# Attention ahead of a mixture of experts: the first two blocks in an order written out, zero products on TensorE, and the output bank put into the rotation

## The chip, the cores and the metric

One core of one Trainium2 chip runs the whole program. The metric is the device time of one execution in microseconds (us), as the median of three runs. Five engines work side by side on the core and meet by semaphores: TensorE (PE, with its weight loads as PEld), VectorE (DVE), ScalarE (ACT), GpSimd (POOL) and SyncE (SP), which issues most of the transfers.

## The reference

Attention with four sink positions and a window of 128 runs over 4 batches, 8 heads, 768 positions and 64 numbers a head. Its output, 3072 rows of 512, goes through eight experts, whose weights for each row come from a gate that is normalised over rows and columns.

```python
scores = scale * np.matmul(q, k.transpose(0, 1, 3, 2))
keep = is_sink | in_window            # 4 sinks, the last 128 positions
scores = np.where(keep, scores, -1e9)
a = np.exp(scores - np.max(scores, axis=-1, keepdims=True))
a = a / (np.sum(a, axis=-1, keepdims=True) + 1e-09)
x = np.matmul(a, v)                   # then reordered to rows of 512

P = np.exp(x @ w_gate - max)          # normalised over rows and columns, 8 times
for e in range(8):
    h = np.maximum(x @ w1[e], 0.0)
    out += P[:, e:e + 1] * (h @ w2[e])
```

## The kernel before

The attention is cut into 24 blocks: four batches of six blocks of 128 queries. A block has eight heads, in two halves of four; half `hh` of block `m` has the number 2m + hh, and "scores 5" below means the second half of block 2. For each half, in this order: TensorE transposes keys and queries (L451), ACT and DVE write them as a high and a low part (`split_qk`, L459 and L460), TensorE multiplies them (`scores`, L482, one bank a head), DVE folds the window (L491) and adds the mask and takes the maximum (L492), ACT takes the exponential (L494), DVE adds and inverts the sums (`scaled`, L500 and L501), POOL scales the four heads (L503), TensorE transposes the result (`transpose_p`, L514), ACT copies it out (PT, L515), POOL cuts a triangle from it (PC, L517), and TensorE multiplies by the values (`values`, L559) into one output bank, O. When both halves are in, the sink part is added (`sink_values`, L567), and `store_x` copies O out, half on ACT (L575) and half on DVE (L576, `xr`). The sinks' own values are written as high and low parts once for each batch (`split_sinks`, L418 and L419, on POOL).

No scheduler moves anything: the order in each engine's queue is the order of the code. The code goes in rounds. In the steady part, round m (from 4 on) holds the scores of block m+1, the values of block m-1, the gate products of an earlier block, the transposes of keys and queries of block m+2 and of the weights of block m, the sinks and the store of block m-1, and last the **fill**: four steps of `plain()`, the first expert's work written as a generator. The fill of a round is either one second-layer product (L640, `plain_g2`, one bank, 12 products of 512 columns) or two first-layer products (L625, `plain_g1`, two banks of 12 products of 256 columns each; call the banks c0 and c1). Each first-layer bank is later read by DVE for the low part of the hidden layer (`h`, L631). Before round 4 there are shorter rounds of half a block each.

TensorE's results go to eight banks. `new_bank` takes the first of the list `banks` and puts it back at the list's end at once, so a bank comes up again eight requests later, and whoever writes it then waits for its last reader. A bank taken with `keep` stays out of the list until it is put back by hand:

```python
    def new_bank(shape, keep=False):
        j = banks.pop(0)
        if not keep:
            banks.append(j)
```

The output bank O is taken that way (L552), and `store_x` puts it back (L572).

After the attention the other seven experts run as products of sums of blocks; that part is not touched.

## Time and profile before

| | |
|---|---|
| median of 3 runs | 2093.32 us (2093.08 to 2093.78) |
| the profiled execution's own time | 2093.69 us |
| its span in the trace | 2091.9 us |
| TensorE busy in the span | 2063.7 us, 99% |
| DVE, ACT, POOL busy | 1473.7, 842.9, 711.7 us |
| the attention with the first expert | from the start to some 260 us |

The span is what the trace shows from the first instruction to the last; 1.8 us of the execution's own time lie around it. TensorE's share of 99% is an average over 2091.9 us: the first 60 us, where the attention starts up and nothing else is there to multiply, look different, and all of TensorE's idle time that matters lies there and at single places of the rounds.

### The profile page before, as it was taken

To read this page: it belongs to the slowest core of one execution; us is meant where nothing else is said; L and a number is where in the kernel's file an instruction comes from. 1 tells how busy PE (TensorE), PEld (TensorE's weight loads), DVE (VectorE), ACT (ScalarE), POOL (GpSimd) and SP (SyncE) were. 2 spreads that over 40 slices of the span, in tenths; PEclk is the share of its full clock that TensorE was granted. 3 is DMA by queue.
4 is the path that set the end of the run, shared out by engine and by line. 5 is a ranking of instruction groups with operands and counts; after the bars stand their busy time and mean duration, and the time that the engine had idled before them with its cause. 6 is when DMAs were issued, how large, how long until landed. Compare 5 with 4: busy or idle time off the path is not lost.

```text
span 2091.9 us, 31617 instructions
## 1 busy us (share of the span) xinstructions
PE 2063.7 (99%) x10561; PEld 1714.7 (82%) x10561; DVE 1473.7 (70%) x2762; ACT 842.9 (40%) x1799; POOL 711.7 (34%) x839
## 2 busy tenths in 40 slices
PE   7999999999999999999999999999999999999998
PEld 6888888888888888888888888888888888888887
DVE  7767697877777776856666666666766666666666
ACT  6877545444444444432233323322432332233222
POOL 6765533332323221332223222323322232223223
PEclk9999999999999999999999999999999999999999
DMA  7655249898989887676666666668766666666662
GB/s 162 155 124 115 87 142 333 292 312 288 321 273 333 274 278 257 236 247 197 203 201 196 201 205 196 201 205 324 235 206 195 198 209 192 201 207 199 196 197 85
DMA packets 397624, 453.82 MB, mean 217 GB/s; under 512 B 99664, under 2 KB 265744, under 8 KB 396560
## 3 DMA queue, kind: packets, MB, share of 16 engines
q1 hardware_dynamic: 397064, 451.57, 68.6%
q8 instruction: 87, 1.43, 0.3%
q14 instruction: 81, 0.66, 0.1%
q10 hardware_dynamic: 392, 0.16, 0.0%
HBM read 314.17 MB, written 137.46 MB: 216 GB/s over the span
## 4 chain that ended last, share of the span: by engine, by line
PE 95%; DVE 3%; ACT 0%; issue 0%; POOL 0%; DMA 0%; SPq 0%; DVEq 0%; POOLq 0%; ACTq 0%
PE c L875 41%; PE o L1439 21%; PE held L1439 8%; PE held L1125 7%; PE o L1125 7%; PE st L625 2%; PE st L640 2%; PE st L559 2%; PE st L482 1%; PE st L451 1%; DVE sc L492 1%; PE st L514 1%; DVE st L491 1%; PE st L567 0%; PE st L591 0%
## 5 line engine op out<-in xcount | busy, mean ns | idle before, releaser
L901 ACT CAST hf<-w 128x512 fp32r<-128x512 f32 x448 | 265.1, 621 | 563.5 <-POOL w L1406 300.7
L1439 PE MATMUL o<-hf,W2q 128*128 128x512 f32 x1920 | 472.1, 390 | 0.0
L1439 PEld LDWEIGHTS o<-hf,W2q 128*128 128x128 f32 x1920 | 360.2, 188 | 75.3 <-DVE acc L1453 0.9
L875 PE MATMUL c<-T,W1q 128*128 128x512 f32 x1530 | 389.0, 390 | 0.2 <-DVE w L1387 0.2
L904 DVE TENSOR_TENSOR hf<-w,hf 128x512 fp32r<-128x512 f32 x448 | 330.6, 766 | 76.6 <-ACT hf L901 69.5
L875 PEld LDWEIGHTS c<-T,W1q 128*128 128x128 f32 x1530 | 286.9, 188 | 60.6 <-DVE w L1387 0.9
L1453 DVE TENSOR_TENSOR acc<-o,acc 128x512 f32<-128x512 f32 x298 | 204.8, 688 | 168.9 <-PE o L1439 168.9
L875 PE MATMUL c<-B,W1q 128*128 128x512 f32 x1134 | 278.4, 390 | 0.0
L1406 POOL TENSOR_TENSOR w<-w 128x512 f32<-128x512 f32 x64 | 82.7, 1292 | 492.5 <-DVE w L1388 492.5
L875 PEld LDWEIGHTS c<-B,W1q 128*128 128x128 f32 x1134 | 212.6, 188 | 43.9
L1387 DVE TENSOR_TENSOR w<-c,M 128x512 f32<-128x512 f32 x192 | 132.4, 689 | 138.4 <-PE c L875 133.9
L1383 ACT COPY M<-c 128x512 f32<-128x512 f32 x192 | 112.8, 587 | 248.1 <-PE c L875 248.0
L1439 PE MATMUL held<-hf,W2q 128*128 128x512 f32 x768 | 194.8, 390 | 0.0
L1125 PE MATMUL held<-W2f,h 128*128 128x512 f32 x672 | 171.2, 390 | 0.0
L875 PE MATMUL c<-T,W1f 128*128 128x512 f32 x672 | 171.0, 390 | 0.1
L1125 PE MATMUL o<-W2f,h 128*128 128x512 f32 x672 | 170.6, 390 | 0.1
L1439 PEld LDWEIGHTS held<-hf,W2q 128*128 128x128 f32 x768 | 144.1, 188 | 29.8
L1421 POOL TENSOR_TENSOR w<-w 128x512 f32<-128x512 f32 x64 | 105.6, 1650 | 176.2 <-DVE hf L904 176.2
L1125 PEld LDWEIGHTS o<-W2f,h 128*128 128x128 f32 x672 | 126.0, 188 | 26.9 <-DVE acc L1132 0.9
L875 PEld LDWEIGHTS c<-T,W1f 128*128 128x128 f32 x672 | 125.9, 188 | 26.6 <-issue 0.5
L1125 PEld LDWEIGHTS held<-W2f,h 128*128 128x128 f32 x672 | 125.9, 188 | 26.4 <-DVE W2f L904 0.5
L1410 POOL TENSOR_TENSOR w<-w 128x512 f32<-128x512 f32 x64 | 83.8, 1309 | 176.3 <-DVE w L1388 172.1
(210 smaller groups left out, 2700.2 us busy)
## 6 DMA issues: line engine op xcount, KB each, us to landing
W2q<-w2s SPq DMA_DIRECT2D x448, 256.0 KB, 3.1
W1q<-w1s SPq DMA_DIRECT2D x444, 256.0 KB, 2.8
w1s<-W1f SPq DMA_DIRECT2D x56, 896.0 KB, 6.8
w2s<-WT SPq DMA_DIRECT2D x136, 256.0 KB, 3.8
r<-in_moe_w_dram SPq DMA_DIRECT2D x64, 512.0 KB, 3.7
w2s<-W2f SPq DMA_DIRECT2D x56, 256.0 KB, 5.4
PB<-psd SPq DMA_DIRECT2D x16, 512.0 KB, 3.7
w2s<-W2f SPq DMA_DIRECT2D x56, 128.0 KB, 6.8
```

The source lines that it names most:

```text
L559: nc.tensor.matmul(O[r * D:(r + 1) * D, c], lhsT=x_[:, 2 * c + r], rhs=y_[:, 2 * c + r], start=(j == 0 and c == 0), stop=(j == len(ops) - ...
L875: nc.tensor.matmul(ps, lhsT=w1(a, k), rhs=x[:, b, k, :], start=(start and j == 0), stop=(stop and j == len(TERMS) - 1), skip_group_check=n ...
L901: nc.scalar.copy(dst[:, 0], src)
L904: low_ = nc.vector.tensor_sub(dst[:, 1], src, f32(dst[:, 0])).ins
L1125: nc.tensor.matmul(o, lhsT=h[c, th][:, a, off:off + P], rhs=W2F[n][:, w, c, :], start=(begin and c == 0 and j == 0), stop=(end and c == 1 ...
L1383: nc.scalar.copy(t, T["c2"])
L1387: nc.vector.tensor_add(w, T["c1"], T[m])
L1406: nc.gpsimd.tensor_sub(S3, T["A11"], T["A21"])
L1410: nc.gpsimd.tensor_add(T["A21"], T["A21"], T["A22"])
L1421: at(k, lambda: nc.gpsimd.tensor_sub(T["A11"], w, T["A11"]))
L1439: nc.tensor.matmul(o, lhsT=W2Q[part, n, m][:, a, k * P:(k + 1) * P], rhs=F[part, n, H_OF[m]][:, w, :], start=(j == 0 and (begin or not hol ...
L1453: nc.vector.tensor_add(sums[m, k], o, sums[m, k])
```

## The change

Blocks 0 and 1, and the scores of block 2's first half, leave the loop over rounds and stand as one sequence ahead of it, in which the values of all four halves and both stores come ahead of scores 4. In this sequence, `idle(k)` issues k products of a zero tile by itself into a bank of its own (`zeros`, kept out of the list until the loop's fourth round). The high and low parts of the sinks are written by DVE and no longer by POOL, for later batches by way of `pending`, which the code empties after the next round's second head. The output bank is taken in turn, without `keep`, where both halves' values stand in one round. Four steps of the fill that stood in the last rounds stand in the loop's first, ahead of its values; the number of steps is the same. `small_products` uses three slots of its bank and not two, and the sums of the gate's rows (`add_up_rows`) come later.

```diff
+    zero = attc.tile([P, P], F32, name="zero")
+    nc.vector.memset(zero, 0.0)
...
     def split_sinks(b):
         VS = seq[b] = att.tile([SK, H * D], F32R, name="VS")
         vmf = vms[b].rearrange("p h d -> p (h d)")
-        nc.gpsimd.tensor_scalar(VS, vmf, 1.0, 1.0, op0=ALU.mult, op1=ALU.mult)
-        nc.gpsimd.tensor_sub(VS[2 * NK:], vmf[2 * NK:], f32(VS[2 * NK:]))
+        nc.vector.tensor_copy(VS, vmf)
+        nc.vector.tensor_sub(VS[2 * NK:], vmf[2 * NK:], f32(VS[2 * NK:]))
...
-    def transpose_qk(m, hh):
+    def transpose_qk(m, hh, gap=0):
...
+                idle(gap * (pr == j == 0))
...
-        t = new_bank([P, HH, P])
+        t = u["pt", hh] = new_bank([P, HH, P])
         for h in range(HH):
             nc.tensor.transpose(t[:, h, :], u["sc"][:, hh * HH + h, SINK:], ident)
-        nc.scalar.copy(u["PT"][0][:, hs], t)
-        if i:
+
+    def copy_p(m, hh):
+
+        u = us[m]
+        hs = slice(hh * HH, (hh + 1) * HH)
+        nc.scalar.copy(u["PT"][0][:, hs], u["pt", hh])
...
-        tsk = new_bank([P, 2, P])
+        tsk = new_bank([P, 3, P])
...
-    def values(m, hh):
+        for j, (t, ls) in enumerate(sums):
+            nc.vector.tensor_copy(Pt[:, t, :], tsk[:, 1 + j, 0:E])
+
+    def values(m, hh, keep=True):
 
         u = us[m]
         if hh == 0:
-            u["O"], u["bank"] = new_bank([P, KC, P], True)
+            u["O"], u["bank"] = new_bank([P, KC, P], True) if keep else (new_bank([P, KC, P]), None)
...
     def store_x(m):
         b, i = spans[m]
-        banks.append(us[m]["bank"])
+        if us[m]["bank"] is not None:
+            banks.append(us[m]["bank"])
...
+    FIRST = 4
...
-    for n in range(-2, 2 * HALF + 1):
-        new_qk = {-2: [0, 1], -1: [], 0: [2, 3]}.get(n, [n + 3])
-        rounds.append(([n + 1] if n >= -1 else [], new_qk, [n] if n >= 0 else [], 2 if n >= 5 else 0, 1 if n >= 1 else 0))
-    rounds.append(([2 * HALF + 2, 2 * HALF + 3], [2 * HALF + 4, 2 * HALF + 5], [2 * HALF + 1], 4, 2))
+    for n in range(FIRST, 2 * HALF + 1):
+        rounds.append(([n + 1], {4: [6], 5: [7, 8]}.get(n, [n + 3]), [n], (4, 0) if n == FIRST else (0, 2), 2))
+    rounds.append(([2 * HALF + 2, 2 * HALF + 3], [2 * HALF + 4, 2 * HALF + 5], [2 * HALF + 1], (0, 4), 2))
     for m in range(HALF + 1, L + 3):
         both = lambda j: [2 * j, 2 * j + 1] if j < L else []
-        rounds.append((both(m + 1), both(m + 2), both(m), {L: 2, L + 1: 2, L + 2: 0}.get(m, 4), 2))
-    begin = {0: 0, HALF + 1: len(rounds) - (L + 2 - HALF)}
-    at_block = lambda m: begin[HALF + 1] + m - HALF - 1
+        rounds.append((both(m + 1), both(m + 2), both(m), (0, {L - 1: 2, L: 2, L + 1: 0, L + 2: 0}.get(m, 4)), 2))
+    at_block = lambda m: len(rounds) - (L + 3 - m)
...
+    zeros = new_bank([P, P], True)
+
+    def idle(k_):
+        for _ in range(k_):
+            nc.tensor.matmul(zeros[0], lhsT=zero, rhs=zero, start=True, stop=True)
+
+    turn_p, score, value, copied_p, cast_qk, total = ((lambda j, f=f: f(*divmod(j, 2))) for f in (transpose_p, scores, values, copy_p, split_qk, scaled))
...
+        idle(5)
+        transpose_qk(0, 0, 1)
+        cast_qk(0)
+        transpose_qk(0, 1, 1)
+        cast_qk(1)
+        score(0)
+        exps(0, 0, 1, 2, 3)
+        score(1)
+        transpose_qk(1, 0)
+        transpose_qk(1, 1)
+        cast_qk(2)
+        mask_sinks(0)
+        exps(1, 0, 1)
+        total(0)
+        exps(1, 2, 3)
+        value_step(0)
+        cast_qk(3)
+        idle(5)
+        score(2)
+        exps(2, 0)
+        total(1)
+        turn_p(0)
+        copied_p(0)
+        exps(2, 1)
+        idle(3)
+        value(0)
+        turn_p(1)
+        exps(2, 2)
+        copied_p(1)
+        value_step(1)
+        score(3)
+        exps(2, 3)
+        load_kq(3)
+        load_kq(4)
+        load_plain_raw(0, 1)
+        load_plain_raw(1, 1)
+        next_piece()
+        exps(3, 0, 1)
+        total(2)
+        exps(3, 2)
+        idle(2)
+        value(1)
+        store_x(0)
+        exps(3, 3)
+        flush(len(pending))
+        high()
+        total(3)
+        transpose_qk(2, 0)
+        turn_p(2)
+        copied_p(2)
+        split_sinks(0)
+        split_p(1, slice(0, H))
+        next_piece()
+        idle(5)
+        turn_p(3)
+        copied_p(3)
+        cast_qk(4)
+        flush(len(pending))
+        value(2)
+        small_products(1, [])
+        load_v(2)
+        idle(2)
+        value(3)
+        sink_values(1)
+        store_x(1)
+        high()
+        score(4)
+        transpose_qk(2, 1)
+        load_kq(5)
+        low()
+        add_up_rows()
+        exps(4, 0, 1)
+        cast_qk(5)
+        exps(4, 2, 3)
+        total(4)
+        for n, (new_s, new_qk, new_p, (ahead, steps), np_) in enumerate(rounds):
+            if n == 3:
+                banks.append(zeros[1])
...
-                    mask_sinks(spans[m][0])
-                    split_sinks(spans[m][0])
+                    pending.append(lambda b=spans[m][0]: split_sinks(b))
...
+                m = new_s[-1] // 2
+                if spans[m][1] == 0:
+                    mask_sinks(spans[m][0])
+            run_fill(ahead)
             flush(len(pending))
             for j in waiting:
-                values(*divmod(j, 2))
+                values(*divmod(j, 2), j + 1 not in waiting)
```

Three places in the queues show what moved. The lists below give line, operation, output, inputs and size; "x2" is two in a row; in brackets stands which engine's or queue's semaphore is waited for. Numbers behind a name tell one buffer's uses apart.

First, TensorE's queue at the end of a round with a first-layer fill, which stores block 5. Before, O is bank `st3`, written last by L567; the fill's banks are `st6` (c0) and `st7` (c1), and `st7` was written last by the gate products:

```order
L567 MATMUL st3_1346<-PS_1234,VS_218 128x128 x4
L625 MATMUL st6_1409<-B11_117,W1_368 128x256 [waits DVE_49,PE_49]
L625 MATMUL st6_1409<-B11_117,W1_368 128x256
L625 MATMUL st6_1409<-B21_118,W1_368 128x256 x2
L625 MATMUL st6_1409<-B11_117,W1_368 128x256 x2
L625 MATMUL st6_1409<-B21_118,W1_368 128x256 x2
L625 MATMUL st6_1409<-B11_117,W1_368 128x256 x2
L625 MATMUL st6_1409<-B21_118,W1_368 128x256 x2
L625 MATMUL st7_1424<-B11_117,W1_368 128x256 [waits Activation_49]
```

After, the same place in such a round; O is `st0`:

```order
L572 MATMUL st0_1214<-PS_1103,VS_436 128x128 x4
L631 MATMUL st6_1283<-B11_117,W1_383 128x256 [waits DVE_49,Activation_49]
L631 MATMUL st6_1283<-B11_117,W1_383 128x256
L631 MATMUL st6_1283<-B21_118,W1_383 128x256 [waits Activation_49]
L631 MATMUL st6_1283<-B21_118,W1_383 128x256
L631 MATMUL st6_1283<-B11_117,W1_383 128x256 [waits Pool_49]
L631 MATMUL st6_1283<-B11_117,W1_383 128x256
L631 MATMUL st6_1283<-B21_118,W1_383 128x256 [waits Pool_49]
L631 MATMUL st6_1283<-B21_118,W1_383 128x256
L631 MATMUL st6_1283<-B11_117,W1_383 128x256 x2
L631 MATMUL st6_1283<-B21_118,W1_383 128x256 x2
L631 MATMUL st0_1298<-B11_117,W1_383 128x256 [waits DVE_49]
```

The second bank of the fill was one that the gate products had used and ACT reads; it is now the output bank of the block being stored, and its first product waits for a DVE instruction.

Second, DVE's queue at block 0's heads. Before, the four heads of the first half (L492 and the one-column read behind it) end with the two small operations on the sums (L500, L501), and the low parts of block 1's keys and queries (L460, with the sink columns, L463) come behind them:

```order
L492 ISA sc_221,st_222<-st0_257,mask0_79 128x132
L492 ISA st_222 128x1
L492 ISA sc_221,st_222<-st1_258,mask0_79 128x132
L492 ISA st_222 128x1
L500 TENSOR_SCALAR st_222<-st_222 128x4
L501 RECIPROCAL st_222<-st_222 128x4
L460 TENSOR_TENSOR KQ0_154<-st2_285,KQ0_154 128x2x2x128
L463 CAST KQ0_154<-KQ0_154 128x4x4
L460 TENSOR_TENSOR KQ1_160<-st3_293,KQ1_160 128x2x2x128
L463 CAST KQ1_160<-KQ1_160 128x4x4
L491 COPY_PREDICATED st5_316<-pick1_94,st5_316 128x128
```

After, the low part of block 1's first half stands behind the fourth head of block 0:

```order
L493 ISA sc_217,st_218<-st6_228,mask0_81 128x132
L493 ISA st_218 128x1
L461 TENSOR_TENSOR KQ0_154<-st4_259,KQ0_154 128x2x2x128
L464 CAST KQ0_154<-KQ0_154 128x4x4
L493 ISA sc_217,st_218<-st7_243,mask0_81 128x132
L493 ISA st_218 128x1
L493 ISA sc_217,st_218<-st1_244,mask0_81 128x132
L493 ISA st_218 128x1
L501 TENSOR_SCALAR st_218<-st_218 128x4
L502 RECIPROCAL st_218<-st_218 128x4
L493 ISA sc_217,st_218<-st2_251,mask0_81 128x132
```

The first half of block 1's operands is made in the middle of block 0's heads, and the second half's behind all of them.

Third, the sinks of a later batch. Before, POOL's queue:

```order
L503 TENSOR_SCALAR sc_1114<-sc_1114,st_1115 128x132 x8
L517 AFFINE_SELECT PC_1217<-PT_1216 128x512 x2
L413 TENSOR_TENSOR vm_1269<-vs_1102,bd_101 96x512
L418 TENSOR_SCALAR VS_1271<-vm_1269 96x512
L419 TENSOR_TENSOR VS_1271<-vm_1269,VS_1271 32x512
L584 TENSOR_TENSOR B12_145<-xr_1240,B12_145 128x2x128
L584 TENSOR_TENSOR B22_119<-xr_1240,B22_119 128x2x128
```

After, DVE's queue holds them, behind the low part of the hidden layer and between two heads of the next block:

```order
L493 ISA st_1325 128x1
L637 SCALAR_TENSOR_TENSOR h00_1282<-st0_1298,h00_1282 128x256
L418 CAST VS_1365<-vm_1212 96x512
L419 TENSOR_TENSOR VS_1365<-vm_1212,VS_1365 32x512
L492 COPY_PREDICATED st3_1334<-pick1_96,st3_1334 128x128
L493 ISA sc_1324,st_1325<-st3_1334,mask1_82 128x132
```

Two operations went from POOL's queue into DVE's, ahead of the third head of a block.

## Rows read from the trace of the kernel before

**Rows 1.** The profile page, its first part: engine, busy us (share of span), instructions.

```profile
PE 2063.7 (99%) x10561; PEld 1714.7 (82%) x10561; DVE 1473.7 (70%) x2762; ACT 842.9 (40%) x1799; POOL 711.7 (34%) x839
```

**Rows 2.** Windows: us, busy PE, PEld, DVE, ACT, POOL, PEclk, DMA share, GB/s.

```profile
24.00:26.00 2.00, 2.00 (x19) 1.29 (x16) 1.37 (x8) 1.32 (x7) 1.70 (x3) 0.50 1.07 271
26.00:28.00 2.00, 2.00 (x14) 1.64 (x14) 0.94 (x3) 1.54 (x5) 1.52 (x5) 0.50 1.19 235
...
36.00:38.00 2.00, 2.00 (x17) 1.56 (x16) 1.33 (x9) 1.32 (x7) 1.58 (x3) 0.50 0.55 130
```

**Rows 3.** What TensorE waited for, 0 to 60 us: total us, times, longest.

```profile
PE st L559 <- ACT PT L515: 2.3, 2, 1.3
PE st L482 <- DVE h L631: 2.3, 2, 1.2
PE st L559 <- POOL PC L517: 1.4, 2, 0.7
PE st L559 <- ACT xr L575: 1.1, 1, 1.1
...
PE st L482 <- DVE KQ L463: 0.6, 1, 0.6
```

**Rows 4.** Timeline, the operations of blocks 0 to 2: start, us, engine, line.

```profile
8.46 0.39 ACT L494 ACTIVATE sc<-sc,st 128x132 f32<-128x132 f32 x1
...
13.45 0.30 DVE L491 COPY_PREDICATED st<-pick,st 128x128 f32<-128x128 int32 x1
...
16.63 0.59 ACT L515 COPY PT<-st 128x512 f32<-128x512 f32 x1
...
16.84 1.42 POOL L503 TENSOR_SCALAR sc<-sc,st 128x132 f32<-128x132 f32 x4 [3.56 <-ACT KQ L459]
...
22.73 0.63 POOL L517 TENSOR_SCALAR_AFFINE_SELECT PC<-PT 128x512 f32<-128x512 f32 x1
```

**Rows 5.** Timeline of TensorE: scores 5 and 8 begin; the first two-bank fill.

```profile
27.17 1.67 PE L482 MATMUL st<-KQ 64*128 64x260 f32 x12
...
45.42 1.75 PE L482 MATMUL st<-KQ 64*128 64x260 f32 x19
...
52.41 3.11 PE L625 MATMUL st<-B,W 128*128 128x256 f32 x24 [0.53 <-DVE st L492]
```

**Rows 6.** Timeline of three rounds: the fill's start on TensorE, DVE's copy of O.

```profile
71.27 2.97 PE L640 MATMUL st<-W2f,h 128*128 128x512 f32 x12
...
72.82 0.42 DVE L576 COPY xr<-st 128x256 f32<-128x256 f32 x1 [0.29 <-ACT xr L575]
...
148.99 3.01 PE L640 MATMUL st<-W2f,h 128*128 128x512 f32 x12
...
151.57 0.42 DVE L576 COPY xr<-st 128x256 f32<-128x256 f32 x1
...
228.97 2.98 PE L640 MATMUL st<-W2f,h 128*128 128x512 f32 x12
...
231.41 0.42 DVE L576 COPY xr<-st 128x256 f32<-128x256 f32 x1
```

**Rows 7.** What TensorE waited for, 60 to 330 us: total us, times, longest.

```profile
PE st L482 <- DVE h L631: 6.7, 9, 0.9
PE st L482 <- DVE acc L650: 1.1, 1, 1.1
```

**Rows 8.** Timeline: the sinks on POOL, a split of weights on DVE, two readers together.

```profile
18.46 0.69 DVE L744 TENSOR_TENSOR W<-r,W 128x512 fp32r<-128x512 f32 x1
...
29.17 1.31 POOL L525 TENSOR_TENSOR dV<-vr 128x512 f32<-128x512 f32 x1 [0.17 <-DMA vr<-in_v_dram]
29.31 1.70 DVE L744 TENSOR_TENSOR W<-r,W 128x512 fp32r<-128x512 f32 x1
...
74.78 0.61 POOL L418 TENSOR_SCALAR VS<-vm 96x512 fp32r<-96x512 f32 x1
75.48 1.27 POOL L419 TENSOR_TENSOR VS<-vm,VS 32x512 fp32r<-32x512 f32 x1
```

More of the change, by code (lines that the diff above doesn't have):

```diff
@@ L274, in tile_sink_attention_moe @@
     one = const.tile([P, 1], F32, name="ones")
+    early = ctx.enter_context(ExitStack())
+    attc = early.enter_context(tc.tile_pool(name="attc", bufs=1))
+    zero = attc.tile([P, P], F32, name="zero")
+    nc.vector.memset(zero, 0.0)
     nc.vector.memset(one, 1.0)
     ones = one.broadcast_to([P, P])
-    early = ctx.enter_context(ExitStack())
-    attc = early.enter_context(tc.tile_pool(name="attc", bufs=1))
     masks = [attc.tile([P, SW], F32, name=f"mask{j}") for j in range(3)]
@@ L294, in tile_sink_attention_moe @@
         nc.gpsimd.affine_select(out=m, in_=m, pattern=[[sign, P]], compare_op=op, fill=0.0, base=0, channel_multiplier=-sign)
-    zero = attc.tile([P, P], F32, name="zero")
-    nc.vector.memset(zero, 0.0)
     NK = H * SINK
@@ L540, in small_products @@
             us[m]["PS"] = att.tile([SK, P], F32R, name="PS")
-        for t, ls in sums:
-            nc.tensor.matmul(tsk[:, 1, 0:E], lhsT=ls, rhs=sel, start=True, stop=True)
+        for j, (t, ls) in enumerate(sums):
+            nc.tensor.matmul(tsk[:, 1 + j, 0:E], lhsT=ls, rhs=sel, start=True, stop=True)
         if m is not None:
             nc.scalar.copy(us[m]["PS"], tsk[0:SK, 0])
-        for t, ls in sums:
-            nc.vector.tensor_copy(Pt[:, t, :], tsk[:, 1, 0:E])
-    def values(m, hh):
+        for j, (t, ls) in enumerate(sums):
+            nc.vector.tensor_copy(Pt[:, t, :], tsk[:, 1 + j, 0:E])
+    def values(m, hh, keep=True):
         u = us[m]
         if hh == 0:
-            u["O"], u["bank"] = new_bank([P, KC, P], True)
+            u["O"], u["bank"] = new_bank([P, KC, P], True) if keep else (new_bank([P, KC, P]), None)
         O = u["O"]
@@ L759, in tile_sink_attention_moe @@
+    at_block = lambda m: len(rounds) - (L + 3 - m)
+    waiting = []
     load_kq(0)
-    waiting, totalled = [], []
-    with tc.manual_schedule():
-        for n, (new_s, new_qk, new_p, steps, np_) in enumerate(rounds):
-            if n == 0:
-                load_kq(1)
-                load_v(0)
-                load_kq(2)
-                load_plain_raw(0, 0)
-                load_v(1)
-                nc.sync.dma_start(wgp[:, :, 0:E], wg.rearrange("(k p) e -> p k e", p=P))
-                add_up_rows()
-            elif n == 1:
-                load_plain_raw(1, 0)
-                mask_sinks(0)
-                split_sinks(0)
-            elif n in (2, 3):
-                load_plain_raw(n - 2, 1)
-            elif n in (at_block(4), at_block(5)):
+    load_kq(1)
@@ new lines, in tile_sink_attention_moe, with exps @@
+    load_v(0)
+    load_kq(2)
+    load_plain_raw(0, 0)
+    load_v(1)
+    nc.sync.dma_start(wgp[:, :, 0:E], wg.rearrange("(k p) e -> p k e", p=P))
+    load_plain_raw(1, 0)
+    zeros = new_bank([P, P], True)
[3 more added lines that the diff above has]
+    turn_p, score, value, copied_p, cast_qk, total = ((lambda j, f=f: f(*divmod(j, 2))) for f in (transpose_p, scores, values, copy_p, split_qk, scaled))
+    def exps(j, *hs):
+        for h in hs:
+            exponential(j // 2, j % 2 * HH + h)
@@ new lines, in low, with high @@
+    def low():
+        while lows:
+            lows.pop(0)()
+    def high():
+        while behind:
+            behind.pop(0)()
+    with tc.manual_schedule():
+        idle(5)
[76 more added lines that the diff above has]
+                banks.append(zeros[1])
+            if n in (at_block(4), at_block(5)):
@@ L805, in tile_sink_attention_moe @@
                     flush(len(pending))
-                    for d in totalled:
-                        scaled(*divmod(d, 2))
-                    totalled.clear()
                 elif c == HH + 1:
```

8 lines of the change are left out of this document (3 added, 5 removed).

## The prediction

> **What bounds the kernel now.** I began with the page's first part [rows 1]: TensorE is busy for 2063.7 of 2091.9 us, DVE for 70%, the others for less. Over most of the program only the amount of TensorE's work counts, and the change leaves that as it is: as many scores, values and fill steps, and some zero products in its waits. So I looked for the 28 us in which TensorE is not busy. The list of what it waited for, cut at 60 us, puts the larger part into the start [rows 3]: 2.3 us for ACT's copies of the transposed weights, 1.4 us for POOL's triangle, 1.1 us for the copy of O, 2.3 and 0.6 us ahead of scores, 7.7 us in five rows. The reader should see that no one engine is late there: one half's work passes through DVE, ACT, POOL, TensorE, ACT and POOL again, and TensorE has nothing else. The windows show a second loss [rows 2]: in 24 to 28 and 36 to 38 us TensorE is busy all the time, at a granted clock of 0.50, that is 1.2 and not 2.4 GHz, each time after a stretch of waiting. Half of these 6.0 us, 3.0 us, would be gone at the full clock.
>
> From 60 us to the end of the attention, the waits are small and regular [rows 7]: 6.7 us in nine waits of scores for the low part of the hidden layer, `h`, and 1.1 us for one addition. Everything else DVE does there is covered by TensorE, and the question for each edit is whether it stays so.
>
> **The change, part by part.**
>
> *The output bank in turn.* The order of TensorE's queue shows that the second bank of a first-layer fill was the gate's bank and is now O's own. Its first product must wait for DVE's copy of O, which before nobody on TensorE waited for in that round. A first-layer fill takes 3.11 us for its 24 products [rows 5]; the second bank begins in its middle, 1.52 us after the fill starts (half of the 3.04 us from its start to the next scores). When is DVE's copy done? In the first round with two full halves the fill starts at 71.27 and the copy ends at 72.82 + 0.42 = 73.24, 1.97 us later; in the round at 148.99 it is 151.99, 3.00 us later; in the last such round, at 228.97, it is 231.83, 2.86 us later [rows 6]. Between these stand 14 more rounds with 1.15 to 3.00 us. DVE's order in a round begins with the heads of new scores, so the copy is late by DVE's own queue and ACT's ahead of it ("0.29 <-ACT xr"), and the lateness starts anew in each round; a stall of TensorE is not won back by the next.
>
> The four steps moved from the end to the front turn the fills round: a round that had a second-layer fill mostly has a first-layer one after. Ten rounds have a first-layer fill and a block to store. I took the gaps of before at the ten (blocks 4 to 20 by their store): 1.97, 2.55, 2.99, 1.64, 1.15, 3.00, 1.66, 1.15, 3.00, 2.86. Seven of them are rounds that before began behind no wait for `h`; after, the 0.87 us wait of the scores goes (6.7 us in 9, the longest 0.9 [rows 7]) and DVE has 0.42 us of work on `h` more (as long as its copy of O, the same number of elements [rows 6]), which makes their gap 0.45 us longer; for the second it is the other way. Less 1.52 us, and never below nothing, the stalls are 0.45, 0.58, 1.47, 0.57, 0.08, 1.93, 0.59, 0.08, 1.93 and 1.79 us: **+9.5 us**. Bounds: nothing, if the copy comes by 1.52 us each time; 17.5 us, if all ten gaps are 3.00 (10 x 1.48 = 14.8, and 7 x 0.45 less 0.45 = 2.7). I take the sum of the rows, since the waiting instruction, its releaser and the releaser's time all stand in them. Behind the waiting product the rest of the fill and the next scores stand, so the stall is paid in full.
>
> *Waits for `h`.* Heads 6 and 7 of the next scores use the fill's two banks before and after. Ten rounds of 0.87 us make 8.7, against 6.7 + 1.1 = 7.8 before [rows 7]: **+0.9 us**.
>
> *The sinks.* POOL's two operations of 0.61 and 1.27 us [rows 8] go to DVE. Half a bank more of DVE's queue comes ahead of heads whose banks the scores wait for. On DVE a subtraction of 512 columns takes 0.69 us [rows 8], and a copy of 512 at most that, at least the 0.42 us of 256 [rows 6]; I take 0.6 and 0.69, 1.3 us a batch. In one of three later batches nothing covers it (1.3), in two a wait for `h` stands there anyway and covers 0.85 (0.45 each), and POOL's shorter queue gives back 0.6: **+1.6 us**, between -0.6 (all hidden) and 4.6 (below).
>
> Row 29.31 in [rows 8] shows such a split at 1.70 us and not 0.69, with a POOL subtraction running from 29.17 for 1.31 us: DVE waits for POOL when both read two tiles. The Trainium skill ("SBUF — State Buffer", section "Who interferes with whom") states it as a lock on the one port pair that both share. The trace agrees at that place. If every split of the sinks met POOL, 1.70 - 0.69 = 1.0 us would come on top for each of the three, 4.6 us for this term and 3.0 us for the sum; I do not take it, since POOL is busy for 34% only.
>
> *The front.* Here I walked the new order with the old durations: per head DVE takes 0.30 for the fold and about as much for the maximum, ACT 0.39; per half POOL 1.42 for the scaling, ACT 0.59 for the copy, POOL 0.63 for the triangle [rows 4]. The low part of block 1's first half now stands between heads of block 0, and ACT's cast behind four exponentials: DVE comes to block 1's first head at 14.3, before at 13.45 [rows 4]. The second half's heads start at about 17.4 as before. But scores 4 now stand behind the values of all four halves and both stores. Block 1's last sums are ready at about 22.5 (eight heads, the copy of O, two splits of weights on DVE); 1.42 us of scaling give 23.9, the transposes, 0.59 of copy and 0.63 of triangle with their hand-overs 26.05, the values and sink products 27.45: scores 4. Before, at 27.17 scores 5 already began [rows 5]. After, scores 5 come at 31.0, scores 6 behind the moved fill at 38.3, scores 7 at 44.6, scores 8 at 49.4, against 45.42 [rows 5]: 4.0 us later, with 3.04 us of fill more done: **+1.0 us**. The zero products come by twos, threes and fives where TensorE's queue waits for another engine by this walk, and cost nothing there; what they keep up is the clock, and TensorE is not what the front then waits for. Were that cover gone, each would cost as long as a transpose of its size. The loads of blocks 3 to 5 stand ahead of their use by a half or more, and no row of [rows 3] names a transfer. Bounds: -10.7 us, if all five waits of [rows 3] and the 3.0 us of low clock go; +4.0, if the fill moved forward gives nothing back.
>
> *The end.* Four steps less in the last rounds; the last gate sums lose some cover: **+0.4 us** (estimate from a copy of 256 columns, 0.42 [rows 6]; at least nothing).
>
> The sum is 9.5 + 0.9 + 1.6 + 1.0 + 0.4 = 13.4 us. The profiled execution took 2093.69 us of its own (span 2091.9), 0.4 above the median; on the median 2093.3 this gives **2106.7 us**. The small slots of `small_products` and the later sums of gate rows are on queues that wait for TensorE in these rows, and cost nothing while POOL is at 34% [rows 1]; without that cover, the same few tenths.
>
> **The rivals.** *Faster: the front saves, and the copy is early.* The written-out order might take the whole 10.7 us, by DVE and ACT never waiting for one another, and the copy of O might come by half of the fill, as it does in two of the ten rounds (1.15 us). Then -10.7 + 0.9 + 1.6 + 0.4 = -7.8 us, 2085.5 us. It decides once the front saves more than 7.1 us with no bank wait (4.2 beyond the 2.9 of the other terms). For it: 7.7 us of waits are there to take. Against it: eight of ten gaps are above 1.52, and the walk finds no shorter chain. The Trainium skill ("TensorE: Matmul & The Clock Gate", Part 1) says that the low clock is the default and activity releases it; [rows 2] agree, 0.50 behind waits, and by that rule the zero products are worth at most the 3.0 us already in this bound. Chance 0.16.
>
> *No change.* The front takes its whole bound and the banks cost theirs: -10.7 + 12.4 = +1.7, 2095.0 us. Or the bank waits are hidden and the front is as walked: 13.4 - 9.5 = 3.9, 2097.2 us. Either is within 0.2% (4.2 us), about what a measurement of this kernel can tell from no change. Chance 0.16.
>
> *Worse.* All ten gaps at 3.00 and the front at +4.0: 17.5 + 0.9 + 1.6 + 4.0 + 0.4 = 24.4 us, 2117.7 us. It decides if the copy in all rounds is as late as in those at 148.99 and 228.97. Chance 0.08.
>
> **How the numbers follow.** My forecast has 0.60, its own range 2100 to 2112 us. It and the worse case are slower (0.68), the others faster (0.16) and the same (0.16). To leave out no more than 2 in 10, the range goes down into the faster case and up past the forecast's end: 2087 to 2113 us.
>
> **What would show it.** In the list of waits from 60 to 330 us, a new row: the first-layer products (now L631) waiting for DVE's copy (L582), eight times or so, about 9 us in all; without it, the largest term is wrong. Scores 8 near 49.4 us, with the two moved fills ahead, would show the walk; below 43 us with as much done, the front saved more than 5 us and my walk is wrong. The low clock between 22 and 39 us should be gone or shorter. The row of waits for `h` should stay within 1 us of 7.8.

## The result and the profile after

The changed kernel takes 2116.41 us as the median of five runs (2114.56 to 2118.74), the kernel before 2093.08 us as the median of five; the ratio is 1.0113, 95% interval 1.0098 to 1.0128. The profiled execution took 2114.56 us with a span of 2112.8 us, 20.9 us longer than the span of before.

The list of what TensorE waited for, 60 to 330 us, of the changed kernel (total us, times, longest), against [rows 7]:

```profile
PE st L631 <- DVE xr L582: 9.4, 7, 1.8
PE st L483 <- DVE h L637: 8.6, 10, 0.9
PE st L451 <- PE st L597: 1.2, 2, 0.6
PE st L483 <- DVE acc L656: 1.1, 1, 1.1
PE st L544 <- POOL sc L504: 0.6, 3, 0.2
```

The first row is new: first-layer products wait for DVE's copy of the output bank, 9.4 us in seven rounds. The third is new as well, 1.2 us. The waits for `h` are about as many as before.

One such round on the timeline, TensorE first and then DVE:

```profile
88.95 1.64 PE L631 MATMUL st<-B,W 128*128 128x256 f32 x12
91.81 1.69 PE L631 MATMUL st<-B,W 128*128 128x256 f32 x12 [1.21 <-DVE xr L582]
93.42 1.47 PE L483 MATMUL st<-KQ 64*128 64x260 f32 x19
```

```profile
89.60 1.29 DVE L461 TENSOR_TENSOR KQ<-st,KQ 128x512 fp32r<-128x512 f32 x2 [0.25 <-ACT KQ L460]
90.80 0.16 DVE L551 COPY Xt<-st 128x8 f32<-128x8 f32 x1
91.33 0.42 DVE L582 COPY xr<-st 128x256 f32<-128x256 f32 x1 [0.37 <-ACT xr L581]
```

The copy ends at 91.75, 2.80 us after the fill began, and the second bank's first product starts at 91.81. From the fill's start to the next scores it is 93.42 - 88.95 = 4.47 us, 1.43 more than the 3.04 us of an unbroken fill, though the idle time shown is 1.21: the stop costs another 0.2 us. These rows have it as longer busy time, 1.64 and 1.69 us for the two halves.

Windows of before and then of after (us, busy PE, PEld, DVE, ACT, POOL, PEclk, DMA share, GB/s), each up to the scores of block 5's first half, the same place in the program:

```profile
0.00:55.45 55.45, 44.10 (x383) 35.70 (x383) 39.44 (x176) 38.10 (x125) 36.98 (x97) 0.91 0.73 166
55.45:257.07 201.62, 192.01 (x2061) 168.01 (x2061) 140.31 (x634) 144.59 (x494) 125.92 (x263) 1.00 0.50 114
```

```profile
0.00:63.65 63.65, 54.20 (x443) 44.25 (x443) 43.19 (x181) 39.29 (x128) 34.72 (x93) 0.92 0.65 143
63.65:277.04 213.39, 192.01 (x2048) 166.78 (x2048) 142.78 (x636) 143.29 (x491) 119.74 (x257) 1.00 0.46 106
```

The second stretch ends at the first product of the gate's normalisation (L34). The front (all that stands ahead of this place) takes 63.65 - 55.45 = 8.2 us more and has 3.04 us of fill more behind it: 5.2 us lost. The rounds take 213.39 - 201.62 = 11.8 us more with twelve fill products less to do: 14.8 us lost. The remaining 0.9 us lie behind. Together 20.9 us.

What the front loses shows on TensorE's timeline of the changed kernel, at its scores and its first fills; [rows 5] have two of the same places of before:

```profile
27.82 0.99 PE L483 MATMUL st<-KQ 64*128 64x260 f32 x12
...
31.00 0.39 PE L483 MATMUL st<-KQ 64*128 64x260 f32 x2 [1.60 <-ACT KQ L460]
...
32.52 4.63 PE L631 MATMUL st<-B,W 128*128 128x256 f32 x24
...
38.99 0.39 PE L483 MATMUL st<-KQ 64*128 64x260 f32 x2 [0.24 <-ACT KQ L460]
...
45.04 0.39 PE L483 MATMUL st<-KQ 64*128 64x260 f32 x1
...
50.70 0.84 PE L483 MATMUL st<-KQ 64*128 64x260 f32 x7
52.82 1.28 PE L483 MATMUL st<-KQ 64*128 64x260 f32 x11 [1.28 <-DVE KQ L461]
54.84 1.02 PE L483 MATMUL st<-KQ 64*128 64x260 f32 x6 [0.75 <-DVE h L637]
```

These are scores 4, 5, 6, 7 and then 8 and 9. The moved fill runs at the lower clock, 1.2 GHz, for its most part (granted clock 0.64 from 32 to 36 us; 4.63 us for 24 products, 3.11 in [rows 5]). At 52.82 the scores wait 1.28 us for the low part of keys and queries. DVE's timeline says why:

```profile
47.66 2.29 DVE L750 TENSOR_TENSOR W2f<-r,W2f 128x512 fp32r<-128x512 f32 x2
...
52.07 0.69 DVE L461 TENSOR_TENSOR KQ<-st,KQ 128x512 fp32r<-128x512 f32 x1
...
54.70 2.33 DVE L750 TENSOR_TENSOR W2f<-r,W2f 128x512 fp32r<-128x512 f32 x2
```

Two pieces of second-layer weights are split in each half round; before it was one (1.14 us at 48.12), and the second-layer products came a round later. Behind these waits the window from 53 to 61 us has a granted clock of 0.57:

```profile
53.00:61.00 8.00, 7.25 (x55) 5.92 (x55) 7.16 (x30) 5.40 (x21) 4.72 (x11) 0.57 0.62 132
```

### The profile page after: what moved, and what is told of

The parts are those of the page before. It is cut to its first block, busy times and chain, and to the rows that moved or that the text cites. A ratio compares the mean times of both kernels' runs of the same rounds, so it can differ in the third digit from the quotient of the medians.

```text
span 2112.8 us, 31704 instructions
## 1 busy us (share of the span) xinstructions
PE 2073.9 (98%) x10609; PEld 1721.6 (81%) x10609; DVE 1478.3 (70%) x2770; ACT 842.9 (40%) x1799; POOL 703.9 (33%) x829
## 3 DMA queue, kind: packets, MB, share of 16 engines
q8 instruction: 87, 1.43, 0.3%
## 4 chain that ended last, share of the span: by engine, by line
PE 93%; DVE 4%; ACT 2%; DMA 1%; issue 1%; POOL 0%; SPq 0%; DVEq 0%; ACTq 0%; POOLq 0%
PE c L968 41%; PE o L1532 20%; PE held L1532 8%; PE o L1218 7%; PE held L1218 7%; PE st L646 2%; PE st L631 2%; PE st L564 2%; PE st L483 1%; DVE sc L493 1%; DVE st L492 1%; PE st L451 1%; PE st L514 1%; ACT KQ L460 0%; ACT sc L495 0%
```

## The experiments

Each time is the median of four or five executions (eleven in the last run of the list). The kernel before was timed beside it on the same chip, with medians of 2091.1 to 2092.3 us; ratios are to that. A diff shows the lines that matter, and "..." stands where others are left out.

**The output bank kept out.** One line of the change undone:

```diff
-                values(*divmod(j, 2), j + 1 not in waiting)
+                values(*divmod(j, 2))
```

> The change with the output bank kept out of the rotation until the store, as before; all else as changed. Theory (the fill's second bank waits for DVE's copy of O): the row of first-layer products waiting for that copy, 9.4 us in 7, goes, and with it some 0.23 us of refilling at each stop (in the round at 88.95 us a wait of 1.21 us made the fill 1.43 us longer): 9.4 + 7 x 0.23 = 11.0 us less than 2116.4, about 2105. Rival (the stall only moves time that other waits would take, for h or in the front): less than 4 us is won, 2113 or more.

2103.11 us, ratio 1.0055 (1.0041 to 1.0068). Its waits from 60 to 330 us are those of the change without the first row:

```profile
PE st L483 <- DVE h L637: 8.6, 10, 0.9
PE st L451 <- PE st L597: 1.2, 2, 0.6
PE st L483 <- DVE acc L656: 1.1, 1, 1.1
```

The theory holds, with 12 to 13 us won; nothing took the wait's place. From the scores of block 5's first half to the gate's normalisation its trace has

```profile
66.43:268.25 201.82, 189.89 (x2048) 166.32 (x2048) 142.86 (x636) 143.20 (x491) 119.79 (x257) 1.00 0.50 113
```

against 213.39 us of the change: 11.6 us less, 9.4 of them idle time and 2.1 busy time. Some 11.5 us over before stay. The front of this run took 66.43 us, though its queues are those of the change up to there:

```profile
0.00:66.43 66.43, 57.70 (x444) 47.74 (x444) 43.43 (x181) 39.39 (x128) 34.61 (x93) 0.85 0.61 136
```

One front took 63.65 us at a mean granted clock of 0.92 and 66.43 at 0.85; such a spread between runs goes into every time below.

**The bank's turn alone, in the kernel before.**

```diff
-            u["O"], u["bank"] = new_bank([P, KC, P], True)
+            u["O"], u["bank"] = new_bank([P, KC, P], True) if keep else (new_bank([P, KC, P]), None)
...
-                values(*divmod(j, 2))
+                values(*divmod(j, 2), j + 1 not in waiting)
```

> The kernel before with nothing changed but the output bank, taken in turn. Theory: its own nine first-layer rounds that scores follow have gaps of 2.55, 2.99, 1.64, 2.58, 2.54, 3.15, 3.15, 2.55 and 3.15 us from the fill's start to the copy's end; less 1.52 this makes 10.6 us of waits, and 9 x 0.23 of refilling, 2.1: about 12.7 us slower than 2093, 2106. Rival (the bank costs only together with the shifted fills): within 3 us of 2093.

2105.38 us, ratio 1.0072 (1.0058 to 1.0085). The row is there in the kernel before as well:

```profile
PE st L626 <- DVE xr L577: 10.1, 8, 1.6
PE st L482 <- DVE h L632: 6.6, 9, 0.9
```

10.1 us of waits for 10.6 forecast, 14 to 15 us in all (by the medians and by the ratio) for 12.7. Eight of the nine waits came within 0.07 us of their own forecast (0.97 us for 1.03, 1.49 for 1.47, 1.57 for 1.63 and so on), and the smallest, 0.12 us, doesn't show. The bank edit is enough by itself. The stretches of its trace, cut at the same places as before:

```profile
0.00:52.71 52.71, 42.21 (x384) 34.35 (x385) 38.23 (x176) 37.93 (x125) 37.47 (x97) 0.94 0.76 173
52.71:266.91 214.20, 194.15 (x2061) 168.51 (x2060) 140.11 (x634) 144.86 (x494) 125.98 (x263) 1.00 0.46 108
```

The rounds take 214.20 - 201.62 = 12.6 us more. The front is 2.7 us shorter than the 55.45 us of before, with the same queues: from 36 to 40 us the granted clock was 1.00 in this run and 0.62 in that of before. So the front of the kernel before varies between runs as well.

**Another bank for the fill.** The output bank stays in turn, but the gate products' bank is drawn ahead of it:

```diff
+            taken = [new_bank([P, P]) for _ in later]
             for j in waiting:
                 values(*divmod(j, 2), j + 1 not in waiting)
...
-                summed.append(gate_products(*g))
+                summed.append(gate_products(*g, taken.pop(0)))
```

> The change with one thing else: the gate products' bank is drawn from the list ahead of the output bank, so that the first-layer fill's second bank is the gate's, which ACT reads early, and the output bank, still taken in turn, goes to the first head of the next scores. Theory (the loss of the bank edit is which bank the fill gets, not that the output bank is in turn): as much is won as by keeping the output bank out, 13.3 us: 2103, and the row of first-layer products waiting for the copy of O is gone. Rival (any turn of the output bank costs): scores wait for the copy in its place, 2110 or more.

2104.57 us, ratio 1.0058 (1.0045 to 1.0072): as much won as by keeping the bank out. The fill's wait is gone, and the scores that now get the output bank wait 0.6 us in two places. So it isn't the turn that costs, but that the fill's second bank became the output bank.

**No zero products.** `idle` issues nothing; the bank stays reserved.

```diff
-        for _ in range(k_):
+        for _ in range(0):
```

> The change without the zero products (the bank stays reserved). Theory (they lie in waits and only keep the clock up; ACT, DVE and POOL set the front): the low clock comes back in parts of the first 30 us, and the time is the same to 3 us longer than 2116.4. Rival (they stand ahead of work that is ready, as the chain of the changed kernel has 0.45 us of them at 25.8 us): 0.5 to 2 us shorter.

2117.81 us, ratio 1.0128 (1.0113 to 1.0144), within the range expected by the theory, but its interval overlaps that of the change: the zero products save 1 to 3 us or nothing, and they don't stand in the way. The low clock came back as expected, 0.57 from 24 to 32 us, where it is 1.00 with them.

**The sinks on POOL again.** `split_sinks` as before.

```diff
-        nc.vector.tensor_copy(VS, vmf)
-        nc.vector.tensor_sub(VS[2 * NK:], vmf[2 * NK:], f32(VS[2 * NK:]))
+        nc.gpsimd.tensor_scalar(VS, vmf, 1.0, 1.0, op0=ALU.mult, op1=ALU.mult)
+        nc.gpsimd.tensor_sub(VS[2 * NK:], vmf[2 * NK:], f32(VS[2 * NK:]))
```

> The change with the sinks' two operations back on POOL. Theory (on DVE they cost 1.6 us): 2114.8 against the 2116.4 to 2117 of the change. Rival (they cost nothing, since the waits for h cover them): the same within 1 us; or POOL is the tighter one in the front and it is slower.

2117.65 us, ratio 1.0119 (1.0103 to 1.0134): nothing won. The move to DVE costs nothing that can be measured. In the changed kernel the two operations stand behind `h`:

```profile
148.44 0.41 DVE L418 CAST VS<-vm 96x512 fp32r<-96x512 f32 x1
148.89 0.68 DVE L419 TENSOR_TENSOR VS<-vm,VS 32x512 fp32r<-32x512 f32 x1
```

**Fill back, one piece.** The four steps return to the last rounds, and the half rounds ahead of scores 8 take one weight piece.

```diff
-(4, 0) if n == FIRST else (0, 2), 2))
+(0, 0) if n == FIRST else (0, 2), 2 if n == FIRST else 1))
...
-{L - 1: 2, L: 2, L + 1: 0, L + 2: 0}
+{L: 2, L + 1: 2, L + 2: 0}
```

> The change with the four fill steps back in the last rounds, and one weight piece and not two in the two half rounds ahead of scores 8 (the moved fill needs the second-layer weights a round earlier, this one doesn't). Theory (the front loses because DVE splits two pieces ahead of the third head, 2.29 and 2.33 us at 47.7 and 54.7, against 1.14 before): the wait of scores 9 for the low part of keys, 1.28 us, shrinks, and the low clock at 54 to 60 us goes; the front's 5.2 us loss falls to about 2, while the bank waits are those of the other rounds (about 12.7 with refilling, not 11.0): about 2114.5. Rival (the written-out sequence itself loses the 5 us): 2117 to 2118.

2119.85 us, ratio 1.0136 (1.0120 to 1.0151): not faster, and slower by 5 us in the ratio, with intervals that overlap. Its bank waits are 11.7 us in eight for 9.4 in seven, as the turned fills would have it. The rest may be the fill that no longer lies in the front's waits; no run shows that part alone. The time expected from the theory didn't come, but the run doesn't clear the pieces, for the clock fell in it. Here is the round from scores 8 to scores 10, in this run, then with one piece (the sequence alone, below) and with two pieces (scores 5 ahead of the values, below), the last two at the full clock:

```profile
52.30:65.20 12.90, 11.17 (x87) 9.59 (x87) 9.30 (x37) 9.00 (x31) 9.18 (x21) 0.74 0.63 134
```

```profile
51.11:61.21 10.10, 8.58 (x86) 7.11 (x85) 8.57 (x35) 8.05 (x29) 7.22 (x18) 1.00 0.83 175
```

```profile
51.64:64.02 12.38, 8.81 (x74) 6.41 (x73) 10.32 (x39) 9.50 (x33) 7.07 (x18) 1.00 0.69 143
```

At the full clock the second piece goes with 2.3 us; with one piece at a clock of 0.74 the round is as long as the change's 12.95 us.

**The sequence alone.** The change with the bank kept out, the sinks on POOL, the fill and pieces as before (the edits above together), so that only the written-out sequence, its zero products and the small moves are left.

> The kernel before with the written-out sequence and its zero products alone: the output bank is kept out, the sinks are on POOL, the fill steps are back in the last rounds, one weight piece stands in the half rounds. Theory (the sequence itself lengthens the front, since scores 4 stand behind the values and stores of blocks 0 and 1 and DVE runs dry): 7 to 9 us slower than before, 2098 to 2100 at a before of 2091. Rival (the front is lost by the other edits, sinks, pieces and moved fill): within 3 us of before.

2104.75 us, ratio 1.0063 (1.0049 to 1.0076), in runs from 2100.13 (mean clock 0.997) to 2107.45 (0.993). The sequence by itself loses, and by more than the 7 to 9 us expected. Its profiled run, the fastest and 4.6 us below the median, on TensorE's timeline at scores 5, 8 and 10:

```profile
32.69 2.18 PE L483 MATMUL st<-KQ 64*128 64x260 f32 x12 [1.60 <-ACT KQ L460]
...
51.11 1.93 PE L483 MATMUL st<-KQ 64*128 64x260 f32 x18
...
61.21 1.35 PE L483 MATMUL st<-KQ 64*128 64x260 f32 x18
```

Scores 5 come 5.5 us after those of before [rows 5], scores 10 5.8 us after (61.21 against 55.45). With one piece the round from scores 8 to 10 takes 10.1 us, as before. Behind scores 10 nothing is lost: from there to the gate's normalisation it takes 201.78 us (61.21 to 262.99), before 201.62.

**Scores 4 ahead of the values of block 1.** In the sequence, for five zero products:

```diff
-        idle(5)
+        cast_qk(4)
+        score(4)
+        transpose_qk(2, 1)
         turn_p(3)
         copied_p(3)
-        cast_qk(4)
+        exps(4, 0, 1)
+        cast_qk(5)
...
-        score(4)
-        transpose_qk(2, 1)
...
-        exps(4, 0, 1)
-        cast_qk(5)
```

> The change with scores 4, the operands of scores 5 and two of block 2's heads moved ahead of the values of block 1 and both stand in the place of five zero products; all else as changed. Theory (DVE and ACT have nothing to do between 22 and 30 us, 2.5 and 2.7 us in two waits, since scores 4 come at 27.8): scores 5 come some 3 us earlier, 3 to 5 us are won: 2112. Rival (the front is bound by the chain of block 1 through POOL and ACT, whatever stands behind it): within 1 us of the change, or slower by the two heads ahead of block 1's copies.

2117.15 us, ratio 1.0117 (1.0101 to 1.0132): nothing won. Scores 4 came at 23.52 but waited 3.01 us for ACT's cast, and scores 5 ran at 31.3 to 34.1 as ever.

**The order of before for blocks 1 and 2,** in two steps, with the bank kept out. First scores 4 between block 1's heads, its cast ahead of the last head, and without the five zero products behind it:

```diff
         store_x(0)
+        cast_qk(4)
         exps(3, 3)
         flush(len(pending))
+        score(4)
+        turn_p(2)
+        copied_p(2)
         high()
         total(3)
...
-        idle(5)
...
-        score(4)
```

> The change with the output bank kept out (as in e1_o_kept), and the sequence put back into the order of before at one place: scores 4, the operands of scores 5 and block 2's heads stand between the heads of block 1 and its values, with the cast for scores 4 ahead of block 1's last head on ACT. Theory (the sequence loses because scores 4 stand behind the values and stores of block 1: in the sequence alone scores 5 begin 5.5 us later than before, and from there on nothing more is lost): scores 5 begin near 28.5 and not 31.7 to 32.7, and 3 to 5 us are won over e1_o_kept, 2098 to 2100 at a before of 2091 to 2092. Rival (other waits of the front take the gain): within 1.5 us of e1_o_kept, 2102 to 2105.

2103.87 us, ratio 1.0056 (1.0042 to 1.0070): as with the bank kept out alone. Scores 5 still began at 31.54, behind the values. So the second step, its diff against the change as well:

```diff
...
+        value(2)
+        exps(4, 2, 3)
         turn_p(3)
         copied_p(3)
-        cast_qk(4)
         flush(len(pending))
-        value(2)
+        score(5)
         small_products(1, [])
         load_v(2)
-        idle(2)
         value(3)
...
-            for j in new_s:
+            for j in new_s[n == 0:]:
```

> As e10_interleaved, and further: the values of block 1's first half ahead of the transposes of its second, and scores 5 ahead of the values of its second half, as before had it. In e10_interleaved scores 5 still began at 31.5, behind all values, so its order was not tested. Theory (what the front loses is how late scores 5 come; from scores 5 on the rounds take as long as before): scores 5 begin near 28.5, and 2 to 4 us are won over e10_interleaved's 2103.9, 2100 to 2102. Rival (the loss is made behind scores 5): within 1 us of it, with scores 5 near 28.5.

2104.11 us, ratio 1.0060 (1.0047 to 1.0074). This time scores 5 did come early on TensorE, and it was no use:

```profile
26.65 0.39 PE L483 MATMUL st<-KQ 64*128 64x260 f32 x1
28.16 1.18 PE L483 MATMUL st<-KQ 64*128 64x260 f32 x11 [1.12 <-DVE st L493]
...
33.38 4.72 PE L631 MATMUL st<-B,W 128*128 128x256 f32 x24 [0.90 <-ACT B L589]
...
39.94 0.38 PE L483 MATMUL st<-KQ 64*128 64x260 f32 x2 [0.24 <-ACT KQ L460]
```

Scores 6 come at 39.94, later than the 38.99 of the change. By its words the rival holds: scores 5 came early, and the loss is made behind them. DVE's timeline shows where the gain went:

```profile
28.47 0.69 DVE L750 TENSOR_TENSOR W<-r,W 128x512 fp32r<-128x512 f32 x1
32.93 0.42 DVE L582 COPY xr<-st 128x256 f32<-128x256 f32 x1 [3.77 <-ACT xr L581]
...
33.56 0.27 DVE L492 COPY_PREDICATED st<-pick,st 128x128 f32<-128x128 int32 x1
```

In DVE's queue block 1's store (L582) stands ahead of the heads of scores 5, and DVE sits idle for 3.77 us until that store can begin, though the products of scores 5 are done at 29.34. So their first head comes at 33.56, as in the change:

```profile
33.62 0.27 DVE L492 COPY_PREDICATED st<-pick,st 128x128 f32<-128x128 int32 x1
```

Before, it came at 28.22, ahead of block 1's store (33.90):

```profile
28.22 0.29 DVE L491 COPY_PREDICATED st<-pick,st 128x128 f32<-128x128 int32 x1 [0.70 <-PE st L482]
```

The run moved scores 5 on TensorE and not their heads on DVE. It shows that an early place on TensorE alone wins nothing; an order with these heads ahead of the store was not run.

**The fill back, in that kernel.** The edit is that of "fill back, one piece".

> As e13_scores5_early, with the four fill steps back in the last rounds and one weight piece in the half rounds. Theory (the moved fill needs two pieces in the half rounds, which make the round of scores 8 and 9 2.4 us longer, 12.45 against 10.1 us at the full clock, and two waits of 0.6 us later, against 3.04 us of cover): within 1 us of e13_scores5_early. Rival (the moved fill fills waits that nothing else fills, as e4_back_one_piece, 3.4 us slower than the change, may say): 2 to 4 us slower than it.

2106.30 us, ratio 1.0066 (1.0052 to 1.0079): 1 to 2 us slower than with the fill moved, between the two expectations, with intervals that overlap. Like the run of the fill back above, it points to a moved fill that gives back a little more than its weight pieces take; neither run is clear of the noise.

**More zero products,** eight ahead of scores 9 and of the values in three rounds, with the bank kept out.

```diff
-            if n == 3:
+            if n == 4:
                 banks.append(zeros[1])
...
+                idle((n == 3) * (j % 2) * 8)
                 scores(*divmod(j, 2))
...
+            idle((n in (1, 2, 3)) * 8)
             run_fill(ahead)
...
```

> The change with the output bank kept out, and more zero products: eight ahead of scores 9 and eight ahead of the values in the three rounds that follow the sequence's first; their bank is held one round longer. Theory (the two waits of 1.28 and 0.75 us at scores 9 let the clock fall to 0.50 from 54 to 60 us, which costs half of that): the low clock there goes and 1 to 3 us are won over e1_o_kept's 2103. Rival (24 + 8 products of 0.05 to 0.1 us stand on the path and the held bank makes a new wait): 0.5 to 2 us lost.

2106.13 us, ratio 1.0065 (1.0051 to 1.0078): the rival's side, 1 to 3 us lost or nothing, at mean clocks of 0.997 to 0.999 for 0.994 to 0.999. In its trace the clock is 1.00 from 32 us on, and eight zero products take 2.05 us at each of the four places, 0.26 us each and not the 0.05 to 0.1 expected. The clock was held and the time was not won.

**Zero products in the kernel before.** Five at the start, six ahead of the values in each of five early rounds.

```diff
+        idle(5)
...
+            if n == 7:
+                banks.append(zeros[1])
+            if 2 <= n < 7:
+                idle(6)
             for j in waiting:
                 values(*divmod(j, 2))
```

> The kernel before with zero products alone: five at the start and six ahead of the values in each of five early rounds, their bank held out until the two-half rounds. Theory (the low clock of before in its first 12 us, at 22 to 28 and 36 to 39 us costs up to half of each, and zero products in waits keep it up): 1 to 3 us faster than before, 2089 to 2091. Rival (one bank less, or products that stand ahead of ready work, cost as much): the same or slower.

2093.91 us, ratio 1.0009 (1.0000 to 1.0018), no gain. The front's row, against the one of before:

```profile
0.00:55.45 55.45, 50.96 (x453) 43.35 (x453) 39.36 (x176) 38.25 (x125) 37.36 (x97) 1.00 0.76 165
```

The granted clock is 1.00 and not 0.91, and several waits of TensorE are gone from its list. But the products also stood ahead of work that was ready: scores 4 begin at 22.60 and not at 18.88. Scores 10 begin at 55.45 in both, so the products cost about what the clock gave back, as the rival has it. The Trainium skill ("TensorE: Matmul & The Clock Gate", Part 1) says that activity releases the low clock; the trace agrees, 1.00 for 0.91.

## Why the prediction was wrong

The direction was right and the time was not: 2106.7 us forecast with 2113 as the upper end, 2116.4 measured. By its own steps:

*The output bank in turn* (+9.5 us): right in mechanism and in the sum of the idle time, 9.4 us in seven rounds. That the sums agree so closely is luck. On the timeline the ten stalls, in the order of the prediction, are 0, 1.21, 1.48, 1.00, 0.47, 1.83, 1.56, 0, 1.84 and 0 us. Four came within 0.1 us; four were together 2.4 us longer than forecast, and two, forecast at 0.45 and 1.79, didn't come. DVE came to the copy earlier or later than the old gaps with a flat 0.45 us would have it; in the run of the bank's turn alone, where the fills stay, nearly every wait was as its own forecast said. The size was also too small by what no row of before showed, the 2.1 us by which the products of the rounds are busy for longer: in the traces the turn is worth 11.6 us (213.39 against 201.82), and keeping the bank out, or giving the fill another bank, wins 12 to 13 us.

*Waits for `h`* (+0.9 us): from the same place on, 8.6 + 1.1 us against 7.9 + 1.1, +0.7. The size came by luck: the prediction let the 1.1 us of the addition go, and they stayed, but it also left out a wait of 1.21 us for `h` at 58.02, which before has between this place and 60 us. Missed were two waits of 0.6 us of the transposes of keys and queries (the row "L451 <- PE st L597", 1.2 us); the profile names a gate product that was done 0.6 us earlier, so that the true releaser was another, which wasn't isolated.

*The sinks* (+1.6 us): wrong, nothing measurable. The prices per operation were near (0.41 and 0.68 us for 0.6 and 0.69), so more was covered than forecast; that the waits for `h` covered them in all rounds is likely and not shown. The dearer price, 1.70 us with POOL reading beside, did not occur there: the four subtractions took 0.68 to 0.74 us. The Trainium skill ("SBUF — State Buffer", section "Who interferes with whom") has such a lock, and no run here shows it at this place.

*The front* (+1.0 us): **the step that failed.** The walk's places were good: scores 4 at 27.82 for 27.45, scores 5 at 31.00 for 31.0, scores 6 at 38.99 for 38.3, scores 7 at 45.04 for 44.6. Scores 8 came at 50.70 for 49.4, 1.3 us late, with the moved fill at 1.2 GHz where the walk had it at 2.4. And the walk stopped there. The round of scores 8 and 9 takes 12.95 us (50.70 to 63.65) and before took 10.03 (45.42 to 55.45): 2.9 us that are in no term. With them go the two weight pieces in place of one, which the prediction did not mention at all (2.3 us at the full clock, from two runs that differ in other things too), and the low clock behind their waits. 1.0 + 1.3 + 2.9 = 5.2.

The 5.2 us are those of the fastest run. With the same queues the front took 66.43 us in the run with the bank kept out, and before's took 52.71 us in the run of the bank's turn alone; by these four fronts the loss is 5.2 to 10.7 us. The low clock between 22 and 39 us, which by the prediction's own sign should be gone or shorter, moved instead. The granted clock is 1.00 from 20 to 28 us (0.62 before), 0.79 from 32 to 40 (0.79 before) and 0.60 from 52 to 60 (1.00 before).

*The end* (+0.4 us): 0.9 us lie behind the rounds.

In the profiled run the sum is 5.2 + 14.8 + 0.9 = 20.9 us for 13.4. Of the 14.8 us, 11.6 are the bank's turn; the other 3.2 hold the waits for `h`, those of the transposes and what no row assigns. The profiled run is the fastest of the five (mean clock 0.997); the others lie at 0.995 to 0.997 and are up to 4 us longer.

Of the rivals, that the front saves 10.7 us was far off; what came is near the worse one's price, but by another way than the one named for it: the copies of the output bank cost less than its ten gaps of 3.00 us, and the front lost more than its 4.0.

What each edit is worth, from the ratios at 2092 us: the bank's turn 12 us in the change (15 in the kernel before, where the fills meet it in other rounds), the sequence alone 13, the moved fill with its pieces -1 to -2 with the bank kept out (-5 with it in turn, bank waits included), the sinks nothing. They add up to the measured 23 to 24; as the runs form one chain from before to the change, that sum is no test of its own.

**What stays open** is why the sequence is slow. It isn't the zero products, and not the place of scores 4 and 5 on TensorE alone. The loss lies ahead of scores 10, and part of it goes with the granted clock. The row of the change's zero products in its front, by line (count, busy us, mean ns, idle before), is this:

```profile
L777 PE MATMUL st<-zero 128*128 128x128 f32 x48 | 8.5, 323 | 1.1 <-DVE zero L278 1.1
```

TensorE's idle time in the front went from 55.45 - 44.10 = 11.4 to 63.65 - 54.20 = 9.5 us, and 8.5 us of zero products came in: the waits are filled, not shorter, and longer by 6.6 us in sum. The mean granted clock of the front is 0.91 before and 0.92 after, though the products held the clock where they stand, to 28 us; it fell behind them. The column doesn't show all of it: it reads 1.00 over the first 12 us of both kernels, while the transposes of keys and queries take 0.42 us each up to 11.1 us before and 0.27 from 5.9 us after. The clock won there was not time won: scores 4 come at 27.82 and not at 18.88, behind the values and stores, as the sequence has them. That DVE's queue sets the pace behind scores 5, by the store of block 1 ahead of block 2's heads, is the best reading of the rows at 32.93 and 33.56 above; no run has tested it.

## What to carry to other kernels

When buffers go round in one list, changing who is kept out of it changes every other user's partner: read from the order of the queues whose last reader the waiting instruction gets, then compare that reader's end with the writer's start in the trace of before. Such a wait can be forecast to 0.07 us, round by round, where the rounds keep their order (the bank's turn alone); where other work moves too, only the sum came out, by luck. Drawing one bank a little earlier repairs it. A walk through a new order has to go on until the old rhythm is reached again, and has to list every small operation that the moved work needs earlier. To test an order, move it in the queues of all engines: scores that come early on TensorE win nothing while their reader's queue has something else first. Work that fills a wait doesn't shorten it.

## What the runs showed that was not expected

A stop of TensorE costs more than its idle time: 1.43 us for a wait of 1.21, 1.70 for one of 1.48 (99.65 to 104.39 us, less 3.04). The spread between runs of one kernel goes roughly with the mean clock: the sequence alone ran at 2100.13 us with 0.997 and at 2107.45 us with 0.993, but the change ran at 2114.56 and at 2117.13 us with 0.997. One and the same front took 63.65 us in one run and 66.43 in another. And 48 zero products in the front left its mean clock where it was, 0.91 and 0.92, while 70 in the kernel before raised it to 1.00 and won no time.
